# Loading keys and queries in runs of four tokens, and spreading them in SBUF

## The chip, the cores and the metric

The kernel runs on one core of one Trainium2 chip. The metric is device time in microseconds (us) of one execution; a run's time is a little longer than the span of its profile, which goes from the first to the last instruction.

## The reference

An attention with a sliding window and ALiBi biases is followed by a feed-forward block with a squared ReLU. The inputs are float32: q, k, v of shape (8, 8, 576, 64), `w_in` of (512, 2048) and `w_out` of (2048, 512).

```python
scores = scale * np.matmul(q, k.transpose(0, 1, 3, 2))        # scale = 1/8
rel = pos[:, None] - pos[None, :]
bias = slopes[:, None, None] * (-np.abs(rel))[None, :, :]     # slopes = 2 ** -(h + 1)
scores = np.where((rel >= 0) & (rel < 128), scores + bias[None], -1e9)
attn = softmax(scores)
x = (attn @ v).transpose(0, 2, 1, 3).reshape(4608, 512)
out = np.maximum(x @ w_in, 0.0) ** 2 @ w_out
```

## The kernel before

**Tiling.** Each batch's 576 tokens are cut into four blocks of 128 tokens and one of 64, so there are 40 blocks (`seq`). Blocks 0 to 7 are the first blocks of the eight batches; they look at no earlier keys. The output of attention is kept transposed in one tile, `xT`, 512 channels (4 x 128 partitions) by 4608 tokens, in bf16. The feed-forward part works on nine groups of 512 tokens. For group 0, `unit` multiplies one block of 128 tokens by two or four 128-wide pieces of `w_in` at a time (L806, tile `h`); groups 1 and 2 take 256 tokens at a time; later groups take all 512 (`fc_step`, L823). ScalarE applies ReLU (L770, `rt`), VectorE squares (L779, `g`), and `o_piece` (L850, `o`) multiplies by `w_out`.

**A block of attention.** Its keys and queries are loaded into a tile `kq` (128 tokens by 2 x 512, bf16), and its values into `vf` or `vt` (L461). Blocks below N_PE are transposed by TensorE into PSUM (L513, `tp`) and copied to `kqf` by VectorE or ScalarE (the helper `copy`, L304 or L306); the others are transposed by a DMA that SP issues (L499, `kqT`). Scores are L633 for blocks 0 to 3, where biases come first by a matmul (L624), and L572 for the others; ScalarE takes the exponential (L641, L596, tile `P`); L676 multiplies by the values (`pv`), VectorE divides (L693, L702, tile `x`). Blocks below N_XP go into `xT` by a TensorE transpose (L722, `xp`) and a copy, the rest by a DMA transpose on SP (L709).

**Loads.** POOL's DMAs cast float32 to bf16 on the way. Keys and queries of blocks 1 to 39 are loaded token by token and head by head (L456): 64 elements, 256 B of float32, in one run, 1024 runs for 128 tokens. Block 0 goes another way (N_HW = 1): SP and ACT load float32 into a tile `stage` in runs of four tokens of one head (1 KB), and VectorE casts and reorders them into `kq` (`cast_kq`). In that layout a partition holds four consecutive tokens `i` of the two heads `r` of a pair; the transposes' results are then put back into the order of tokens by the copy from PSUM:

```python
src = st.tile[:, 0:512].rearrange("p (i g c) -> p c g i", i=4, c=C)[:, c0:c1]
o = o.rearrange("p c (g i) -> p c g i", i=4)
```

The weights come in five pieces of `w_in` (2, 2, 4, 4 and 4 of 128 columns; i0 to i4 in the list FIRST, L401) and four of `w_out` (o0 to o3, L404). FIRST gives the order in which POOL issues these and the blocks' loads: `k3` is keys and queries of block 3, `v3` its values.

**Order.** Every piece of work is a task with the engines that can do it, a key and the ring buffers it takes. `Plan.order` runs through a cost model of durations and latencies and fixes on which engine, and in which order, each task is emitted; on the chip each engine works through its list in that order and waits by semaphores. ADJ adds offsets to the keys of single tasks, LEAD says how far ahead of need attention blocks are due, SLACK adds reserves to DMA landings, NEAR lets a task with a smaller key pass one that is ready earlier. Where TensorE is expected to wait early on, `fill` puts in matmuls on a tile of zeros (L285), and N_WARM more stand at the start (L483).

Of the kernel before, what the change touches and what calls it, by code (L numbers as in the profile page):

```python
# [13 lines left out]

FIRST = ["k0", "k1", "i0", "v0", "v1", "k2", "v2", "k3", "v3", "i1", "o0", "i2", "i3", "i4", "o1", "o2", "o3", "k4", "k5", "v4", "k6", "k7", "v5", "v6", "v7"]
DIAG = [[0], [1], [2], [3], [4, 5], [6, 7]]
N_HW = 1
N_PE = 8  # L20
N_XP = 8
N_CUT = 0
N_PVH = 2
N_WARM = 8
HALVED = [(7, 1), (7, 2), (7, 3)]
N_EV = 4
SLACK = {"kq": 0.0, "kqT": 4500.0, "v": 2000.0, "x": 2500.0}
FILL = 0.7
LEAD = 1200
IOTA = 3  # L30
TP, XP = "h", "h"

# [5 lines left out]
DUE = {m: 200.0 * m - 1e5 for m in range(40)}  # L38

ADJ = {  # L40
    "b3": 8899994.7, "e13.1": 299208.63, "e14.1": 388.4, "e6.3": -698571.67, "e8.1": 100925.31, "ev1.0.0": 399002.11,
    "ev2.1.2": -197151.21, "fc3.10": -299530.23, "fc3.11": 199489.0, "fc3.13": -99828.3, "fc3.3": -201022.2,
    "fc3.4": -99975.3, "fc3.5": -98590.21, "o0.2.3": -299655.64, "o1.0.1": 99368.6, "o1.0.3": -394556.77,
    "o1.3.0": 199256.6, "o1.3.1": -9000017.0, "o1.3.2": -197810.54, "o1.3.3": 401.7, "o2.0.0": 99409.71,
    "o2.1.0": -790.13, "o2.1.2": -198747.1, "o2.2.2": 603810.31, "o2.2.3": 101596.66, "o2.3.0": -393446.03,
    "o2.3.2": 297555.78, "o3.0.0": 80, "pv20.0": 599.54, "r11.1": -954.05, "r12.0": -864.77, "relufc3.1": -398899.93,
    "reluu0.0.0": -301007.9, "reluu0.0.1": -99855.3, "reluu0.2.0": -197840.0, "reluu2.0.7": 496046.89,
    "s12": -100922.05, "s13": 40, "s17": 1287.08, "s4": -778.4, "s6": -98770.15, "s8": 5078.93,
    "squ0.0.1": -600103.44, "squ0.2.0": -100094.3, "squ1.1.6": -8498736.06, "tp4.0": -2659.55, "u0.0.1": 400493.27,
    "u0.0.2": 200, "u0.0.3": 198055.18, "u1.0.1": -398247.52, "u1.0.4": -955.31, "u1.1.0": -198342.1,  # L50
    "u1.1.2": -296084.77, "u1.1.4": -200120.3, "u1.1.6": -199431.2, "u1.1.7": -8597648.05, "u2.0.0": 393881.15,
    "u2.1.1": -98247.04, "xp7.0": 99135.7,
}


# [23 lines left out]
class Plan:  # L79
# [6 lines left out]
    LAND = {"POOL": 2400.0, "SP": 2200.0, "ACTQ": 900.0}  # L86
    TO_SP = 600.0
    LANES = 8
    NEAR = {"PE": 25, "ACT": 250, "DVE": 0}
    FILL_UNTIL = 30000.0  # L90

    def __init__(self, bufs):
# [114 lines left out]
def kernel(  # L207
# [53 lines left out]
    def ring(name, n, shape, dt=BF16):  # L261
        return [const.tile(shape, dt, name=f"{name}_{i}") for i in range(n)]
# [4 lines left out]
             "kqT": ring("kqT", size["kqT"], [128, 2 * C, 128]), "kqT0": ring("kqf", B, [128, 2 * C, 128])}  # L267
    Pt = ring("P", size["P"], [128, H, 2, 128])
    xt = ring("x", size["x"], [128, d_model])
    stages = ring("stage", min(2, N_HW), [128, 2 * d_model], FP32)  # L270

    psum_bufs = {"h": 2, "o": 2, "a": 4}
    plan = Plan({**psum_bufs, "rec": 4, "rt": 3, "g": 2, "osb": 3, "v0": B, "kqT0": B, "stage": 2, **size})

    def bank(slot, name):
        slot.tile = psum.tile([128, 512], FP32, tag=slot.tag, bufs=psum_bufs[slot.tag], name=name)
# [13 lines left out]
    def act(n):  # L290
        return n * 0.832 + 51.0
# [117 lines left out]
        else:  # L409
            t_wout[n] = t  # L410

    s_kq, s_v, t_kq, t_v = {}, {}, {}, {}

    def source(t, m, split=False):
        b, kb = seq[m]
# [5 lines left out]
    def load_block(m, key, v_key=None):  # L421
        kb = seq[m][1]
        n = blk[kb]
        ns = 870.0 * n / 128
        split = m < N_HW
        s_kq[m], s_v[m] = Slot("kq"), Slot("v" if kb else "v0")

        def view(t, i):
            o = t[0:n, i * d_model:(i + 1) * d_model]
            return o.rearrange("s (r e) -> s r e", r=2) if split else o.rearrange("s (h d) -> s h d", h=H)  # L430

        if split:
            s_st = Slot("stage")
            t_l = []
            for i, src in enumerate((k, q)):
                for r, (eng, e) in enumerate((("SP", nc.sync), ("SP", nc.sync) if m else ("ACTQ", nc.scalar))):
                    def fetch(i=i, src=src, r=r, e=e):
                        e.dma_start(view(stages[s_st.idx], i)[:, r], source(src, m, split)[:, :, r])
                    t_l.append(plan.add({eng: 740.0}, key + 0.1 * i, fetch, [], [] if t_l else [s_st], dma=330.0,
                                        lat=(1100.0 if m else 1500.0) + 600.0 * (r if m else i * (1 - r)),  # L440
                                        name=f"l{'kq'[i]}{m}.{r}", after=t_l[0] if t_l else None))

            def cast_kq(i):
                w = slice(i * d_model, (i + 1) * d_model)
                copy((c_k, c_q)[i],
                     kq[s_kq[m].idx][:, w].rearrange("s (i r d) -> s r i d", i=4, d=D),
                     stages[s_st.idx][:, w].rearrange("s (r i d) -> s r i d", r=2, d=D))
            engs = {"DVE": 350.0, "ACT": 480.0} if m else {"DVE": 350.0}
            c_q = None
            c_k = plan.add(engs, key, lambda: cast_kq(0), t_l[0:2], [s_kq[m]], name=f"ck{m}")  # L450
            c_q = plan.add(engs, key, lambda: cast_kq(1), t_l[2:4] + [c_k], [], [s_st], name=f"cq{m}")
            t_kq[m] = [c_k, c_q]
        else:
            def fetch_kq():
                for i, src in enumerate((k, q)):
                    nc.gpsimd.dma_start(view(kq[s_kq[m].idx], i), source(src, m, split))  # L456
            t_kq[m] = [plan.add({"POOL": 1780.0}, key, fetch_kq, [], [s_kq[m]], dma=2 * ns,
                                name=f"lkq{m}", count=2, slack=SLACK["kq"] if m >= N_PE else 0.0)]

        def fetch_v():  # L460
            nc.gpsimd.dma_start(tile_of(s_v[m])[0:n, :, 0:D], source(v, m))  # L461
        l_v = plan.add({"POOL": 890.0}, key + 0.2 if v_key is None else v_key, fetch_v, t_zero if kb == HALF else [], [s_v[m]],
                       dma=ns, name=f"lv{m}", after=t_kq[m][-1] if m >= B else None,
                       slack=SLACK["v"] if m >= B else 0.0)
        t_v[m] = [l_v] + ([t_one["v0", m]] if m < B else [t_one["v", i] for i in range(size["v"])])
# [26 lines left out]
    def transpose_kq(m, due):  # L492
        n = blk[seq[m][1]]
        kb = seq[m][1]
        sT = s_kqT[m] = Slot("kqT" if kb else "kqT0")
        split = m < N_HW
        if m >= N_PE:
            def flip():
                nc.sync.dma_start_transpose(out=tile_of(sT)[:, :, 0:n], in_=kq[s_kq[m].idx][0:n, :])  # L499
            t_f = plan.add({"SP": 1500.0}, due - 60, flip, t_kq[m] + (t_zero if kb == HALF else []), [sT],  # L500
                           [s_kq[m]], dma=1700.0 * n / 128, name=f"kqT{m}", slack=SLACK["kqT"])
            t_kqT[m] = [t_f]
            return
        t_tp, evs = [None, None], [[], []]
        for i in range(2):
            st = Slot(TP if m else "o")

            def tp(i=i, st=st):
                fill(t_tp[i], bank_of(st, "tp"))
                st.tile = st.tile.bitcast(BF16)  # L510
                src = kq[s_kq[m].idx][:, i * d_model:(i + 1) * d_model]
                for j in range(C):
                    nc.tensor.transpose(st.tile[:, j * 128:(j + 1) * 128],  # L513
                                        src[:, j * 128:(j + 1) * 128], ident)
            t_tp[i] = plan.add({"PE": 4 * mm(128)}, due - 60 + i, tp,
                               [t_ident, t_tp[0] if i else last["tp"], t_kq[m][min(i, len(t_kq[m]) - 1)]],
                               [st] if i else [st, sT], [s_kq[m]] if i else [], name=f"tp{m}.{i}")

            pieces = [(0, C // 2), (C // 2, C)] if m < N_EV else [(0, C)]
            for c0, c1 in pieces:  # L520
                def evac(i=i, st=st, c0=c0, c1=c1, e=len(evs[i])):
                    o = tile_of(sT)[:, i * C + c0:i * C + c1, 0:n]
                    if split:
                        src = st.tile[:, 0:512].rearrange("p (i g c) -> p c g i", i=4, c=C)[:, c0:c1]
                        o = o.rearrange("p c (g i) -> p c g i", i=4)
                    else:
                        src = st.tile[:, 0:512].rearrange("p (c s) -> p c s", c=C)[:, c0:c1, 0:n]
                    copy(evs[i][e], o, src)
                w = (c1 - c0) * n
                evs[i].append(plan.add({"ACT": act(w), "DVE": dve_p(w, 1 if split else 2)}, due - 58, evac,  # L530
                                       [t_tp[i]], [], [st], name=f"ev{m}.{i}.{c0}"))
        last["tp"] = t_tp[1]
        t_kqT[m] = evs[0] + evs[1]
# [384 lines left out]
```

The softmax here doesn't subtract the row's maximum and nothing guards it: scores larger than these inputs give would overflow.

## Time and profile before

| | us |
|---|---|
| four runs, median (lowest to highest) | 313.83 (313.48 to 315.04) |
| the profiled execution | 314.52 |
| its span | 312.7 |
| TensorE busy | 307.0 |
| VectorE, ScalarE, GpSimd busy | 165.8, 169.4, 106.2 |

In the views below, PE is TensorE, PEld its weight loads, DVE VectorE, ACT ScalarE, POOL GpSimd and SP SyncE. A table by windows has for each stretch its length, then the busy time of PE, PEld, DVE, ACT and POOL with the number of instructions in brackets, the granted clock of TensorE, the mean occupancy of the DMA engines (over 1 where packets overlap) and GB/s. A chain of waits has start, length and what ran. A DMA line has the issuing queue, the number of issues, the KB that one writes and the median us from issue to landing; the KB are those of bf16, so that a load reads twice as many.

### The profile page before, as it was taken

Reading aid. Unit: us, or ns where it says so; the run is one execution under the profiler, and the core shown is the slowest. Engines: PE = TensorE matmul, PEld = TensorE weight load, DVE = VectorE, ACT = ScalarE, POOL = GpSimd, SP = SyncE. Lnnn points to the kernel's source line nnn. Section 1 sums busy time; section 2 is a strip of 40 time slices with the busy share of each in tenths; the row PEclk is TensorE's granted clock in tenths of the full one; section 3 lists DMA queues with packets and bytes.
Section 4 is the critical chain, followed back from the end, with each engine's and each line's share of the span. In section 5 each row is a group of like instructions: output and inputs, shape, how many; then the busy total and the mean of one; then the engine's idle time right before and its main releaser. Section 6 shows DMA issues by size and latency. Waiting matters only on the chain.

```text
span 312.7 us, 7098 instructions
## 1 busy us (share of the span) xinstructions
PE 307.0 (98%) x2792; PEld 175.0 (56%) x2792; DVE 165.8 (53%) x496; ACT 169.4 (54%) x324; POOL 106.2 (34%) x132
## 2 busy tenths in 40 slices
PE   8999999999999999999999999999999999999996
PEld 4579757686686844555455554555444444444443
DVE  5664357367667546878677665878222222222211
ACT  2686445486685545864597756665443443434400
POOL 8933596364660943703737364000000000000000
PEclk9999999999999999999999999999999999999999
DMA  9999999999999999998999999941110100011122
GB/s 129 162 205 206 174 194 171 155 141 165 172 188 163 143 173 198 148 125 175 140 179 157 170 163 175 193 78 52 52 34 38 63 36 34 36 36 34 34 85 84
DMA packets 166290, 39.54 MB, mean 126 GB/s; under 512 B 156400, under 2 KB 161776, under 8 KB 166256
## 3 DMA queue, kind: packets, MB, share of 16 engines
q0 software_dynamic: 115184, 18.10, 86.0%
q1 hardware_dynamic: 50640, 20.65, 37.4%
q8 instruction: 22, 0.36, 0.5%
q10 hardware_dynamic: 432, 0.33, 0.4%
q14 instruction: 12, 0.10, 0.1%
HBM read 36.70 MB, written 9.44 MB: 148 GB/s over the span
## 4 chain that ended last, share of the span: by engine, by line
PE 90%; DMA 4%; POOL 4%; issue 0%; ACT 0%; POOLq 0%
PE o L850 40%; PE h L823 27%; PE h L806 12%; PE pv L676 6%; PE s L572 5%; DMA w_in_sb<-in_moe_w_in_dram 4%; POOL kq L456 2%; POOL vf L461 1%; POOL w_in_sb L401 1%; PE tp L513 1%; PE xp L722 0%; POOL w_out_sb L404 0%; POOL dist L320 0%; ACT osb L306 0%; POOLq L320 0%
## 5 line engine op out<-in xcount | busy, mean ns | idle before, releaser
L850 PE MATMUL o<-w_out_sb,g 128*128 128x512 bf16 (+2 forms) x592 | 141.8, 374 | 0.1
L770 ACT ACTIVATE rt<-h 128x512 bf16<-128x512 f32 (+1 forms) x145 | 86.1, 601 | 89.3 <-PE h L823 69.9
L779 DVE TENSOR_TENSOR g<-rt 128x512 bf16<-128x512 bf16 (+1 forms) x145 | 60.4, 419 | 95.8 <-ACT rt L770 95.3
L823 PE MATMUL h<-xT,w_in_sb 128*128 128x512 bf16 x384 | 96.8, 380 | 0.4 <-DMA xT<-x 0.4
L850 PEld LDWEIGHTS <-g 128*128 128x128 bf16 x592 | 54.2, 98 | 57.1 <-issue 0.2
L596 ACT ACTIVATE P<-s 128x512 bf16<-128x512 f32 x120 | 62.2, 607 | 12.9 <-PE s L572 12.8
L823 PEld LDWEIGHTS <-w_in_sb 128*128 128x128 bf16 x384 | 35.4, 98 | 40.4 <-DMA xT<-x 0.5
L456 POOL DMA_DIRECT2D kq<-in_k_dram x39 | 33.6, 861 | 41.5 <-DMA kqT<-kq 31.9
L806 PE MATMUL h<-xT,w_in_sb 128*128 128x128 bf16 (+1 forms) x512 | 46.2, 246 | 0.1
L604 DVE TENSOR_TENSOR P<-P,masks 128x512 bf16<-128x512 bf16 x96 | 38.6, 419 | 11.6 <-ACT P L596 9.1
L806 PEld LDWEIGHTS <-w_in_sb 128*128 128x128 bf16 x512 | 39.0, 98 | 5.5 <-DMA w_in_sb<-in_moe_w_in_dram 0.3
L461 POOL DMA_DIRECT2D vt<-in_v_dram x32 | 27.3, 853 | 32.8 <-PE pv L676 31.7
L456 POOL DMA_DIRECT2D kq<-in_q_dram x39 | 33.6, 860 | 9.1 <-DMA w_out_sb<-in_moe_w_out_dram 3.7
L702 DVE TENSOR_TENSOR x<-pv,rec 128x256 bf16<-128x256 f32 (+1 forms) x80 | 32.1, 418 | 0.8
L676 PEld LDWEIGHTS <-P 128*128 128x128 bf16 (+1 forms) x576 | 24.2, 101 | 11.3 <-DVE g L779 1.3
L676 PE MATMUL pv<-vt,P 128*128 128x65 bf16 (+1 forms) x448 | 22.8, 194 | 0.0
L304 DVE COPY osb<-o 128x512 f32<-128x512 f32 (+1 forms) x19 | 13.0, 685 | 17.2 <-PE o L850 12.0
L306 ACT ACTIVATE osb<-o 128x512 f32<-128x512 f32 (+1 forms) x18 | 10.4, 579 | 21.5 <-PE o L850 21.5
L572 PEld LDWEIGHTS <-kqT 64*128 64x128 bf16 x448 | 12.4, 94 | 7.6 <-issue 7.2
L693 DVE RECIPROCAL rec<-pv 128x4 f32<-128x4 f32 (+1 forms) x80 | 12.4, 172 | 6.2 <-PE pv L676 5.4
L572 PE MATMUL s<-kqT 64*128 64x128 bf16 (+1 forms) x256 | 15.6, 210 | 0.0
L572 PE MATMUL s<-kqT,kqT 64*128 64x128 bf16 (+1 forms) x192 | 11.4, 210 | 0.0
(46 smaller groups left out, 104.7 us busy)
## 6 DMA issues: line engine op xcount, KB each, us to landing
out_dram<-osb SPq DMA_DIRECT2D x28, 256.0 KB, 5.4
kq<-in_k_dram POOLq DMA_DIRECT2D x31, 128.0 KB, 7.0
kq<-in_q_dram POOLq DMA_DIRECT2D x31, 128.0 KB, 7.5
vt<-in_v_dram POOLq DMA_DIRECT2D x24, 128.0 KB, 7.6
w_out_sb<-in_moe_w_out_dram POOLq DMA_DIRECT2D x4, 512.0 KB, 17.3
out_dram<-osb SPq DMA_DIRECT2D x14, 128.0 KB, 2.3
w_in_sb<-in_moe_w_in_dram POOLq DMA_DIRECT2D x3, 512.0 KB, 13.4
vf<-in_v_dram POOLq DMA_DIRECT2D x8, 128.0 KB, 7.0
```

The costliest lines, as they stand in the source:

```text
L456: nc.gpsimd.dma_start(view(kq[s_kq[m].idx], i), source(src, m, split))
L461: nc.gpsimd.dma_start(tile_of(s_v[m])[0:n, :, 0:D], source(v, m))
L572: nc.tensor.matmul(sS[2 * g2 + r].tile[:, jj * 256 + c0:jj * 256 + c0 + w], tile_of(s_kqT[mk])[rows, c, :], tile_of(s_kqT[mq])[rows, C + c ...
L596: nc.scalar.activation(flat(Pt[sP.idx]), sS[i].tile.rearrange("p (j t) -> p j t", j=2)[:, :, lo:hi], AF.Exp, bias=0.0, scale=scale)
L604: nc.vector.tensor_tensor(flat(Pt[sP.idx]), flat(Pt[sP.idx]), flat(masks), op=ALU.mult)
L676: nc.tensor.matmul(sv.tile[0:n, hi * (D + 1):(hi + 1) * (D + 1)], prob, tile_of(s_v[mk])[:, h, 0:D + 1], start=mk == parts[0][1], stop=mk ...
L702: nc.vector.tensor_tensor(o, heads(sv)[0:n, :, 0:D], sr.tile[0:n, :].unsqueeze(2).to_broadcast([n, 4, D]), op=ALU.mult)
L770: nc.scalar.activation(srt.tile[:, 0:n], slot.tile[:, 0:n], AF.Relu, bias=0.0, scale=1.0)
L779: nc.vector.tensor_tensor(o, i, i, op=ALU.mult)
L806: nc.tensor.matmul(slot.tile[:, f * w:(f + 1) * w], w_in_sb[:, cc, fc * 128:(fc + 1) * 128], xT[:, cc, lo:lo + w], start=cc == 0, stop=cc ...
L823: nc.tensor.matmul(slot.tile, w_in_sb[:, cc, fc * 128:(fc + 1) * 128], xT[:, cc, g * 512:(g + 1) * 512], start=cc == 0, stop=cc == C - 1)
L850: nc.tensor.matmul(slot.tile[:, 0:hi - lo], gt[:, fc, t * 128:(t + 1) * 128], w_out_sb[:, fc, lo:hi], start=fc == 0, stop=fc == FCB - 1)
```

## The change

Keys and queries of blocks 1 to 7 (N_ROW = 8) are loaded by POOL in runs of four tokens of one head, 1 KB of float32 each, 256 runs for a block's keys and 256 for its queries. They land as bf16 in columns of `xT` from 1536 on, which attention writes later (`rows_of`), and VectorE or ScalarE copies them to `kq` in two spreads of 128x512 (`spread`). Block 0's `stage` is also laid into `xT`. The copies from PSUM of blocks 1 to 5 now put tokens back in order, as block 0's do. N_PE goes from 8 to 6, so that blocks 6 and 7 are transposed by DMA. That transpose keeps the order by groups of four tokens and head pairs, and nothing behind it puts the tokens of blocks 6 and 7 back: the scores of these two blocks are taken between tokens and heads in another order, with the same shapes and instructions. The order of the first loads, SLACK, LEAD, NEAR, ADJ and two counts (N_EV, how many early blocks have their copies from PSUM halved; N_PVH, how many blocks keep `pv` in the `h` banks) are also different.

```diff
-FIRST = ["k0", "k1", "i0", "v0", "v1", "k2", "v2", "k3", "v3", "i1", "o0", "i2", "i3", "i4", "o1", "o2", "o3", "k4", "k5", "v4", "k6", "k7", "v5", "v6", "v7"]
+FIRST = ["k0", "v0", "k1", "k2", "i0", "i1", "v1", "v2", "k3", "i2", "i3", "v3", "o0", "o1", "i4", "o2", "k4", "o3", "k5", "k6", "v4", "k7", "v5", "v6", "v7"]
-N_PE = 8
+N_PE = 6
+N_ROW = 8
-N_PVH = 2
+N_PVH = 1
-N_EV = 4
-SLACK = {"kq": 0.0, "kqT": 4500.0, "v": 2000.0, "x": 2500.0}
+N_EV = 3
+SLACK = {"kq": 0.0, "kqT": 4000.0, "v": 1000.0, "x": 3000.0}
-LEAD = 1200
+LEAD = 480
 ADJ = {
...
-    NEAR = {"PE": 25, "ACT": 250, "DVE": 0}
+    NEAR = {"PE": 0, "ACT": 60, "DVE": 25}
...
-    stages = ring("stage", min(2, N_HW), [128, 2 * d_model], FP32)
+    def stage():
+        return xT[:, 0, NT - 4 * d_model:].bitcast(FP32)
+
+    def rows_of(m, i):
+        c, z = (m % 3 + 1, m // 3) if m < 6 else (0, 2)
+        end = NT - (2 * z + 1 - i) * d_model
+        return xT[:, c, end - d_model:end]
...
-        split = m < N_HW
+        split = m < N_ROW
...
+        elif split:
+            def fetch_rows():
+                for i, src in enumerate((k, q)):
+                    nc.gpsimd.dma_start(rows_of(m - 1, i).rearrange("s (r e) -> s r e", r=2), source(src, m, split))
+            t_l = plan.add({"POOL": 1560.0}, key, fetch_rows, [], [s_kq[m]], dma=1320.0, name=f"lkq{m}", count=2)
+
+            def spread(i):
+                copy(t_kq[m][i],
+                     kq[s_kq[m].idx][:, i * d_model:(i + 1) * d_model].rearrange("s (i r d) -> s r i d", i=4, d=D),
+                     rows_of(m - 1, i).rearrange("s (r i d) -> s r i d", r=2, d=D))
+            t_kq[m] = []
+            for i in range(2):
+                t_kq[m].append(plan.add({"DVE": dve(512, 2), "ACT": act(512)}, key, lambda i=i: spread(i),
+                                        [t_l] + t_kq[m][:1], name=f"c{'kq'[i]}{m}"))
...
-        split = m < N_HW
+        split = m < N_ROW
         if m >= N_PE:
             def flip():
                 nc.sync.dma_start_transpose(out=tile_of(sT)[:, :, 0:n], in_=kq[s_kq[m].idx][0:n, :])
```

## The prediction

> **What bounds the kernel now.** I read the page first: who is busy, and when.
>
> ```profile
> PE 307.0 (98%) x2792; PEld 175.0 (56%) x2792; DVE 165.8 (53%) x496; ACT 169.4 (54%) x324; POOL 106.2 (34%) x132
> ...
> PE   8999999999999999999999999999999999999996
> ```
>
> TensorE is the bound from end to end, at a clock of 1.0 throughout, so time can only come from work that TensorE no longer does or from time that it spends idle or on filler at the start. The table by windows says where that is, first for all of TensorE, then for the filler of L285 alone:
>
> ```profile
> 10.00:14.00 4.00, 3.46 (x50) 2.43 (x49) 3.14 (x11) 1.72 (x4) 4.00 (x7) 1.00 2.43 154
> 14.00:18.00 4.00, 3.66 (x52) 2.49 (x51) 2.30 (x9) 3.78 (x12) 2.78 (x4) 1.00 1.58 195
> 18.00:22.70 4.70, 4.60 (x64) 3.53 (x62) 3.58 (x20) 3.96 (x15) 1.93 (x3) 1.00 1.24 206
> ...
> 100.00:295.00 195.00, 194.61 (x1586) 98.86 (x1586) 102.14 (x297) 107.50 (x196) 48.21 (x59) 1.00 1.00 108
> ...
> 10.00:14.00 4.00, 1.23 (x13) 0.76 (x13) 1.00 2.43 154
> ```
>
> Behind 100 us only 0.4 us is idle, ahead of the tail. Early "busy" flatters, since the modelled ends overlap, so I count work instead: instructions times the step of a dense run, from the chain that ended last:
>
> ```profile
> 26.56 6.43 PE h L806 x112
> 32.99 0.86 PE o L850 x4
> ...
> 38.23 0.45 PE tp L513 x8
> ...
> 42.58 0.55 PE s L572 x16
> ...
> 46.84 0.37 PE pv L676 x12
> ```
>
> That is 57 ns for an `h` of 128 columns, 216 for a 512-wide `o` or bias, 56 for a transpose, 34 for a score, 31 for a `pv`. By the timeline of TensorE, these were issued before 12.36 us: 16 transposes of keys and queries (0.90), 6 biases (1.30), 16 scores (0.55), 16 pv (0.50), 4 transposes of x (0.22), in all 3.5 us; 8.9 us were lost. From 12.36 to 22.70, where the first long run of `h` begins: 16 tp (0.90), 2 biases (0.43), 16 s (0.55), 16 pv (0.50), 12 xp (0.67), 48 h (2.75), 8 o (1.72), in all 7.5 of 10.3 us; 2.8 us were lost. From 22.70 TensorE runs dense.
>
> What it waits for there is data. The chain is POOL issuing loads without a gap from 1.34, and then a load:
>
> ```profile
> 13.11 13.40 DMA w_in_sb<-in_moe_w_in_dram
> 26.52 0.04 issue
> 26.56 6.43 PE h L806 x112
> ```
>
> **The change, part by part.** *Size of the row loads.* The DMA views of short windows give single landings:
>
> ```profile
> w_in_sb<-in_moe_w_in_dram POOLq DMA_DIRECT2D x1, 256.0 KB, 5.8
> ...
> kq<-in_q_dram POOLq DMA_DIRECT2D x1, 128.0 KB, 5.1
> ...
> w_in_sb<-in_moe_w_in_dram POOLq DMA_DIRECT2D x1, 256.0 KB, 7.3
> vf<-in_v_dram POOLq DMA_DIRECT2D x1, 128.0 KB, 7.1
> ```
>
> With issue starts of 3.23, 2.36, 10.91 and 10.04, the two small w_in pieces land 1.52 and 1.07 us after the load ahead of them. They are written in the runs of 512 B that the new loads would have, and carry twice the data: 0.54 to 0.76 us for a key or query load. Today's land 0.83 to 0.84 apart. POOL's issue is 0.77 for such a w_in piece against 0.87 to 0.95 for a kq load, so issue alone would hold loads to 0.77. I take 0.76: 0.08 us for each of six early loads, 0.5 us in all; the other end is 0.3 each, 1.8 us. The Trainium skill (DMA: Bandwidth & Descriptors, section "Why small descriptors are slow") charges a fixed few cycles for each descriptor; my estimate from its formula is 0.66 us for a load, which would double the 0.5.
>
> *Order of the loads.* This is worth more. With 6.68 us for the first landing (as now), 0.76 for a row load, 0.87 for a v, 1.3 for a small w_in (between 1.07 and 1.52) and 2.55 for a large weight piece (w_in 2 lands at 23.26, 2.55 behind w_out 0), the new list lands: v0 6.7, k1 and q1 8.2, k2 and q2 9.7, i0 11.0, i1 12.3 (now 18.2), v1 13.2 (now 10.8), v2 14.1 (13.3), q3 15.6 (15.0), i2 18.2 (23.3), i3 20.7 (26.5), v3 21.6 (17.1), o0 24.1 (20.7). Block 0 is no earlier: its x waits for q0, which comes by SP and ACT as now, so the 8.9 us stay. From 12.4 TensorE has 16 h for block 0 in place of 8, and at 13.2 + 2.6 = 15.8 block 1's x (from vf's landing at 10.77 to the end of x's copy at 13.9 it is 3.1 now, partly waiting for engines). Between 12.4 and 15.8 the work is 16 h, 4 tp, 8 s, 2 biases, 16 pv: 2.4 of 3.4 us. From 15.8 to 18.2 there are 32 h, 8 xp, 8 tp, 8 s and 2 biases: 3.4 us for 2.4. With i2 at 18.2 it stays dense: 48 h (2.7 us) carry it past i3 at 20.7, and 48 more to 24.6, past o0. So 1.0 us is lost by this count; I take 1.4, because engines will not be free at each moment. Gain 2.8 - 1.4 = 1.4 us; ends 0 and 2.8. What is late next is block 3's x (v3 at 21.6 plus 3), covered by the 96 h of i2 and i3, and behind 24.1 by w_out 0's parts.
>
> *N_PE 8 to 6.* Blocks 6 and 7 lose 16 transposes on TensorE: 16 x 56 ns = 0.9 us, and every one lies in dense time. In their place SP issues two DMA transposes, landing 6.8 us later in the median, 10.5 at worst before 70 us. With q7 landing near 41 they are there by 52; from scores to x takes 5.6 us now (49.1 to 54.7), so 58, and u1.1 needs them near 62 (64.5 now). Cost nothing; without that cover of 4 us, what is missing. On SP the stores of the first group queue behind them: three osb buffers hold that.
>
> *Spreads.* 14 copies of 128x512 bf16, SBUF to SBUF. Nearest rows: 602 ns for VectorE's cast of the same layout from f32, 597 for ScalarE's copy, 417 for VectorE's bf16 copy from PSUM, 272 for a memset with no input. I take 0.42: 2.5 us for the six early ones, ends 1.6 and 3.6. The evictions of blocks 1 to 3 also scatter: 425 ns on VectorE, as block 0's do, for 280 to 290 now; at most 12 x 0.14 = 1.7. Between 5 and 20 us VectorE idles 5.7 us and ScalarE 5.7 (busy 9.3 of 15 each), so I cost both at nothing on the path: k2 and q2 come 2.7 us earlier. Without that cover it is the slower rival below.
>
> *Spreads against POOL.* Beside VectorE's cast (6.28 to 6.89) POOL's issue took 0.93, its neighbours 0.92 to 0.96, a quiet one 0.87: so 0.06 us lost each, 0.4 for six, under the rounding of my loss. The Trainium skill (SBUF — State Buffer, section "Who interferes with whom") speaks against this change: a VectorE copy in a two-port mode shuts GpSimd out for its whole length. By that rule six spreads could hold up issues by 2.5 us and take the early gain.
>
> *LEAD, SLACK, NEAR, ADJ, N_EV, N_PVH.* They only reorder. They can win at most the 0.4 us of idle time; the longest late TensorE wait is 0.4 us (for x by DMA transpose), and four like it would cost 1.6. Taken as 0.
>
> Sum: 1.4 + 0.9 = 2.3 us. The profiled execution took 314.52 us for a span of 312.7, and 313.83 is the median; its span would become 310.4, the median 313.83 - 2.3 = **311.5**.
>
> **The rivals.** *B, the order gives nothing back:* v1 comes 2.4 us later, so block 1 is late and i1 has only block 0 to feed. For it: block 0 and 1 alone fill 12 to 16 us. Then only the transposes count: 313.83 - 0.9 = 312.9 (312.3 to 314.2).
>
> *C, slower: VectorE and ScalarE become the bound from 8 to 20 us.* ScalarE is already busy 3.78 of 4 us from 14 to 18. Spreads and scattered evictions (2.5 + 1.7 = 4.2 us) land in the chain of each block. Shared by both engines and all on the path they cost 2.1 us, in one queue 4.2; with no early gain and less the 0.9 this is 1.2 to 3.3 us, 315.0 to 317.1, middle 316.1. It decides once block 2's x copy, which starts at 18.22 now, starts after 20.
>
> *D, the run is not merged:* packets stay as small as now, rows land 0.83 apart, and only order and transposes count: 0.5 less, 312.0.
>
> **How the numbers follow.** My forecast 0.62 (its own range 309.6 to 312.3), B 0.19, C 0.15, D 0.04. A measurement can tell about 0.5%, 1.6 us, from no change: faster is below 312.3, slower above 315.4. The forecast and half of D are faster, 0.64; B and the rest of D and a little of C within, 0.22; most of C slower, 0.14. For 8 in 10 the range runs from 309.4 (2.8 + 0.9, and the idle 0.4 with rounding) to 315.4, where C's lower part is in.
>
> **What would show it.** Right: the first long run of h starts near 18 us in place of 22.70, filler behind 12 us is nearly gone, L513 has 48 transposes in place of 64, kq loads land below 0.8 us apart, TensorE is still at 1.00 with under 1 us of idle time after 30 us. Wrong: x copies of blocks 1 and 2 behind 16 and 18 us, POOL's issues over 1.1 us beside spreads, or new TensorE waits for kqT or x by DMA after 50 us.

## The result, and the profile after

The kernel after takes 315.10 us in the median of 38 runs (313.48 to 319.10), the kernel before 313.42 in 57 (312.94 to 315.75). The ratio, in which strongly disturbed runs are left out, is 1.0045, with an interval of 1.0033 to 1.0058: slower by 0.45%, a small change, but one that its interval sets apart from none. The forecast was 311.5.

The profiled execution took 314.79 us for a span of 312.56. Its page, the lines of busy time and of TensorE in 40 slices:

```profile
PE 305.4 (98%) x2754; PEld 173.4 (55%) x2754; DVE 171.7 (55%) x502; ACT 170.2 (54%) x326; POOL 103.9 (33%) x132
...
PE   8799999999999999999999999999999999999995
```

TensorE has 38 instructions fewer (16 transposes and 22 fillers), and its first slices are not fuller than before. The same stretches as before, by windows (columns: length, then the busy time of PE, PEld, DVE, ACT and POOL with counts, PEclk, DMA share, GB/s):

```profile
4.58:10.00 5.42, 4.42 (x41) 3.20 (x40) 2.70 (x14) 1.91 (x5) 5.42 (x8) 1.00 1.52 186
10.00:14.00 4.00, 3.36 (x48) 2.56 (x48) 2.63 (x8) 2.92 (x7) 3.75 (x5) 1.00 1.85 177
14.00:18.00 4.00, 3.36 (x52) 2.19 (x50) 3.30 (x13) 3.94 (x14) 2.18 (x4) 1.00 1.25 206
18.00:22.70 4.70, 4.65 (x81) 4.16 (x79) 2.14 (x15) 4.35 (x16) 2.14 (x3) 1.00 1.46 198
```

The DMAs move more (206 for 195 GB/s from 14 to 18 us), but TensorE is busy for less. ScalarE has 3.94 of 4 us from 14 to 18.

**The data did come earlier.** The early row loads land 0.67 to 0.73 us apart (forecast 0.76, before 0.83). The second small piece of `w_in`, i1, lands at 12.16 us (forecast 12.3, before 18.21), i2 at 18.44 (18.2; 23.26), i3 at 20.60 (20.7; 26.52). All of this part of the forecast held.

**TensorE did not gain by it.** By 30 us both profiled executions have begun the same work: 174 `h`, 8 `o`, 32 transposes of keys and queries, 16 of x, 8 biases, 32 scores and 32 `pv`. The rows of `h` up to 30 us, before and after (count, then busy us, mean ns, idle us before):

```profile
L806 PE MATMUL h<-xT,w_in_sb 128*128 128x128 bf16 x174 | 10.5, 219 | 0.1
```

```profile
L830 PE MATMUL h<-xT,w_in_sb 128*128 128x128 bf16 x174 | 11.1, 219 | 0.2
```

Counted as in the prediction (instructions times the step of a dense run), TensorE has then lost 11.8 us in both: in the kernel after 0.4 more between 5 and 10 us, 0.6 less between 10 and 15, and 0.4 more between 15 and 20. Up to 30 us no load is on the chain that ended last. Pieces of it (start, length, what ran):

```profile
9.22 0.24 PE tp L537 x4
9.46 0.02 issue
9.48 0.44 DVE kqf L314
9.92 0.02 issue
9.94 0.39 ACT kqf L316
10.33 0.04 issue
10.37 0.29 PE pv L700 x4
```

Block 1's first transposes, then the two halves of their copy one behind the other, then the second `pv` of block 0: TensorE stands 0.73 us for ScalarE's half. The transposes take a bank of `h`, which has two, and with N_PVH = 1 block 0's `pv` takes the next from there; a bank comes free when its last half is copied.

**Balance of the two profiled executions.** TensorE ends at 309.38 in place of 309.83: 0.9 us of transposes less, 0.45 more lost in small pieces from 30 to 240 us. From the last matmul to the end of the span it is 3.18 us, before 2.83; outside the span 2.23, before 1.86. So -0.45 + 0.35 + 0.37 = 0.27, and 314.79 - 314.52 is 0.27. The medians lie further apart (1.7 us) because the runs of the kernel after spread more: a quarter lie below 314.08 and a quarter above 316.04 (before 313.22 and 313.91). Before's profiled execution was one of its long ones. Of the 38 runs 26 have a mean granted clock above 0.998, and their median is 314.3 us; the other 12 have 316.9. So about half of the 1.7 us is there at full clock too: 0.9, of which 0.35 is the tail and 0.4 the time outside the span.

### The profile page after: what moved, and what is told of

It is laid out like the page before. It is cut to its first block, busy times and chain, and to the rows that moved or that the text cites. A ratio compares the mean times of both kernels' runs of the same rounds, so it can differ in the third digit from the quotient of the medians.

```text
span 312.6 us, 7033 instructions
## 1 busy us (share of the span) xinstructions
PE 305.4 (98%) x2754; PEld 173.4 (55%) x2754; DVE 171.7 (55%) x502; ACT 170.2 (54%) x326; POOL 103.9 (33%) x132
## 4 chain that ended last, share of the span: by engine, by line
PE 93%; DMA 3%; ACT 2%; DVE 1%; issue 0%
PE o L874 38%; PE h L847 27%; PE h L830 14%; PE pv L700 6%; PE s L596 5%; DMA xT<-x 3%; PE wm L507 1%; ACT kqf L316 1%; DVE kqf L314 1%; PE tp L537 1%; PE xp L746 0%; PE s L648 0%; PE tp L295 0%; ACT P L665 0%; PE s L657 0%; ACT masks L354 0%
## 5 line engine op out<-in xcount | busy, mean ns | idle before, releaser
L628 DVE TENSOR_TENSOR P<-P,masks 128x512 bf16<-128x512 bf16 x96 | 40.0, 421 | 15.4 <-ACT P L620 11.6
L480 POOL DMA_DIRECT2D kq<-in_k_dram x32 | 26.9, 840 | 54.2 <-DMA kqT<-kq 44.5
L700 PEld LDWEIGHTS <-P 128*128 128x128 bf16 (+1 forms) x576 | 23.2, 100 | 11.0 <-ACT P L665 1.0
L480 POOL DMA_DIRECT2D kq<-in_q_dram x32 | 27.2, 849 | 0.9 <-DMA vt<-in_v_dram 0.8
L700 PE MATMUL pv<-vt,P 128*128 128x65 bf16 (+1 forms) x448 | 21.5, 194 | 0.0
L314 DVE COPY osb<-o 128x512 f32<-128x512 f32 (+1 forms) x18 | 12.3, 683 | 13.4 <-PE o L874 9.8
L596 PEld LDWEIGHTS <-kqT 64*128 64x128 bf16 x448 | 12.4, 94 | 7.8 <-issue 7.4
L717 DVE RECIPROCAL rec<-pv 128x4 f32<-128x4 f32 (+1 forms) x80 | 12.4, 172 | 6.6 <-PE pv L700 5.7
```

The costliest lines, as they stand in the source:

```text
L596: nc.tensor.matmul(sS[2 * g2 + r].tile[:, jj * 256 + c0:jj * 256 + c0 + w], tile_of(s_kqT[mk])[rows, c, :], tile_of(s_kqT[mq])[rows, C + c ...
L628: nc.vector.tensor_tensor(flat(Pt[sP.idx]), flat(Pt[sP.idx]), flat(masks), op=ALU.mult)
L700: nc.tensor.matmul(sv.tile[0:n, hi * (D + 1):(hi + 1) * (D + 1)], prob, tile_of(s_v[mk])[:, h, 0:D + 1], start=mk == parts[0][1], stop=mk ...
```

## The experiments

The theory after the result (*S*): the early gain was spent on the way to TensorE, in spreads and scattered copies. Rivals: the order of the loads, the DMA transposes of blocks 6 and 7, and the later order of tasks.

**With a new plan.** In the first four kernels the planner makes a new order for each setting.

*Rows and spreads, but the lists and knobs of before:*

```diff
-FIRST = ["k0", "v0", "k1", "k2", ...
+FIRST = ["k0", "k1", "i0", "v0", ...
-N_PE = 6
+N_PE = 8
...
```

(and so N_PVH, N_EV, SLACK, LEAD, NEAR and ADJ)

> The changed kernel's row loads and spreads, with every list and knob of the kernel before (FIRST, N_PE = 8, N_PVH, N_EV, SLACK, LEAD, NEAR, ADJ). Before is 313.4 us, after 315.1. Theory S (spreads and scattered copies from PSUM lengthen each early block's chain, so that TensorE loses what the earlier data gave): 314 to 315.5, with block 1's first transpose of keys over 1 us later than the 7.6 us of before. Theory O (the new order and knobs cost the time, the rows themselves help): 312.5 to 313.4. Theory C (in some runs TensorE's clock is halved for a window, for want of filler): runs with a mean clock below 1.000 appear only where filler is much less than the 40 instructions of before.

320.46 us, ratio 1.022 (1.0204 to 1.0235). A wait of 1.2 us for x by DMA transpose opens; it ends at 89.6 us.

*After with tokens in place of rows:*

```diff
-N_ROW = 8
+N_ROW = 1
```

> The changed kernel with N_ROW = 1: token by token loads as before, no spreads, and transposes of blocks 6 and 7 by DMA in the order of tokens; all other lists and knobs as after. Theory S: at or below before, 312.3 to 313.4, since the new order keeps its 1.4 us and N_PE = 6 its 0.9. Theory O: as after, 314.5 to 315.5. Theory C: follows the number of filler matmuls, not the loads.

324.61 us, 1.0359 (1.0342 to 1.0376).

*After with eight blocks transposed by TensorE:*

```diff
-N_PE = 6
+N_PE = 8
```

> The changed kernel with N_PE = 8, so that TensorE transposes blocks 6 and 7 and their tokens stand in order. By my price for 16 transposes in dense time it is 0.9 us slower than after (316.0). If instead the DMA transposes cost more than they save, it is 315.1 or less.

323.02 us, 1.0304 (1.0288 to 1.032). Up to 30 us its TensorE loses what after's does (11.8 us). Behind that, as in the token kernel, waits open from 83 to 85 us on, the longest for x (2.0 us, up to 90.1, here), and the clock is halved (from 89.0 to 95.8 us here). For the token kernel, first the longest wait of TensorE (us in total, times, longest), then its windows, the clock third from the end:

```profile
PE h L830 <- DMA xT<-x: 3.4, 1, 3.4
```

```profile
84.00:88.00 4.00, 2.64 (x43) 1.64 (x41) 3.26 (x10) 3.34 (x7) 2.84 (x4) 1.00 3.32 111
88.00:99.00 11.00, 7.23 (x61) 4.81 (x62) 4.53 (x13) 4.39 (x8) 3.31 (x4) 0.53 1.71 174
```

*The kernel just above without spreads* (`t_kq[m] = [t_l]`): the transposes read the rows where they landed, 64 columns for each head:

```diff
+                    if N_HW <= m < N_ROW:
+                        for r in range(2):
+                            at_c = r * 256 + j * D
+                            nc.tensor.transpose(st.tile[r * D:(r + 1) * D, j * 128:(j + 1) * 128],
+                                                rows_of(m - 1, i)[:, at_c:at_c + D], ident)
```

> As e3, but without the 14 spreads: each 128x128 transpose of blocks 1 to 7 becomes two of 64 columns that read the landed rows in place, 112 in place of 56. Theory S: below e3 by 1 us or more, less 0 to 1.6 us for the added transposes (28 to 56 ns each), so 314 to 315.5, with block 1's first transpose at most 0.7 us behind the landing of its keys. Theory O: no better than e3, 316 or above.

318.01 us, 1.0154 (1.0128 to 1.018). A pair of 64-column transposes takes the 56 ns of one of 128, but what follows a group of them starts later. The group and the next instruction, in this kernel and in the kernel after:

```profile
16.47 0.41 PE L533 MATMUL tp<-ident,xT 128*64 128x128 bf16 x8
16.82 0.30 PE L699 MATMUL pv<-vf,P 128*128 128x65 bf16 x4
```

```profile
16.44 0.39 PE L537 MATMUL tp<-ident,kq 128*128 128x128 bf16 x4
16.67 0.59 PE L648 MATMUL s<-slopes,ident 128*128 128x512 bf16 x2
```

That is 0.35 us for 0.23, some 0.12 us for each group, which the expectation of a later kernel without spreads takes for nothing. What follows from the four: ADJ and the lists fit one plan only; another plan costs 4.6 to 11 us against the kernel before, over half of it lost between 80 and 100 us (2.9 to 9.9 us by the count above, where before loses 0.1). They say little of rows and spreads, so the next kernels hold the order of every task and change only what a task issues.

**With the order held.** *After's order, token loads, no spreads, plain copies:*

```diff
-                    nc.gpsimd.dma_start(rows_of(m - 1, i)..., source(src, m, split))
+                    nc.gpsimd.dma_start(kq[s_kq[m].idx][:, i * d_model:(i + 1) * d_model]..., source(src, m))
             def spread(i):
-                copy(...)
+                pass
```

> After's order of every instruction on every engine kept as it is; only what is emitted differs: keys and queries of blocks 1 to 7 come token by token into kq, no spreads, copies from PSUM dense (so blocks 6 and 7 keep the order of tokens). e1 to e3 let the planner order anew and lost 5 to 11 us, most of it near 85 to 95 us, so order has to be held. Theory S (spreads and scattered copies eat what the earlier data gives): 314.0 to 315.1, the start of h for 8 to 10 us of feed-forward work within 0.5 us of after's 18.8 to 19.1. Theory R (row loads are needed for this order): that start moves past 20 us and the time to 316 or more.

316.97 us, 1.0115 (1.0088 to 1.0141), some 1.9 us above the kernel after. But the early part is not where they go. `w_in` lands later (i2 at 19.16 for 18.44, i3 at 21.66 for 20.60), and TensorE stands 0.4 us for i2 and 0.5 us for v3; the plain copies (0.36 us, below) and a start 0.14 us earlier offset part of this. In sum it is not behind. The same run of `h` starts, here and in the kernel after (counts up to 30 us):

```profile
27.44 2.73 PE L829 MATMUL h<-xT,w_in_sb 128*128 128x128 bf16 x46
```

```profile
27.48 2.73 PE L830 MATMUL h<-xT,w_in_sb 128*128 128x128 bf16 x46
```

So up to there the rows with all that goes with them gain nothing over tokens, and Theory R's late start does not come. Behind it this profile has one long wait of TensorE, up to 86.8 us; why it is there is not shown:

```profile
PE h L829 <- DMA xT<-x: 2.3, 1, 2.3
```

*After's order, no spreads for blocks 1 to 5*, 64-column transposes as above:

```diff
             def spread(i):
+                if m < N_PE:
+                    return
```

> After's order kept; the ten spreads of blocks 1 to 5 are left out, and TensorE transposes the landed rows in pieces of 64 columns (28 ns each in e4, so no dearer). Blocks 6 and 7 as in after. Theory S: 0.5 to 1.5 us below after, 313.6 to 314.6, and the time outside the span, 2.2 us in the three kernels with spreads and 1.8 in the three without, falls back to 1.8. If spreads lie beside other work: 315.1 as after.

315.20 us, 1.0058 (1.0034 to 1.0081): not faster. TensorE's waits (engine, tile and line; us in total, times, longest) are those of the kernel after (0.7, 0.5 and 0.5):

```profile
PE pv L708 <- ACT kqf L316: 0.7, 1, 0.7
PE s L665 <- DVE kqf L314: 0.5, 1, 0.5
PE pv L708 <- ACT P L673: 0.5, 1, 0.5
```

Its shortest run is longer than after's (314.91 for 313.48), about by what its ten groups of 64-column transposes add (1.2 us at 0.12 each). So leaving the spreads out leaves TensorE's waits as they are: they are not on after's path, and that part of *S* falls.

*Before's order with rows, and VectorE spreads just ahead of the transposes;* the copies from PSUM of blocks 1 to 7 scatter, here and in the next kernel:

```diff
+                    if m < N_ROW:
+                        nc.gpsimd.dma_start(rows_of(m - 1, i)..., source(src, m, True))
...
+                if N_HW <= m < N_ROW:
+                    nc.vector.tensor_copy(kq[s_kq[m].idx]..., rows_of(m - 1, i)...)
```

> Before's order kept; keys and queries of blocks 1 to 7 come in runs into xT, VectorE spreads each just ahead of its transposes, copies from PSUM scatter. Theory S: 0.5 to 2 us slower than before, 313.9 to 315.4. Theory O (only the new order costs): at or below before, 312.6 to 313.4, by 0.5 us of earlier landings.

318.41 us, 1.0145 (1.0121 to 1.017).

*Before's order with rows, no spreads:* the first of these two edits, scattered copies, and 64-column transposes as above.

> As f3 without spreads, transposes by 64 columns from the landed rows. Theory S: faster than f3 by 0.5 to 1.5 us and than before by 0 to 0.7 us, 312.7 to 313.4; only the scattered copies are left as a cost. Theory O: as f3.

314.88 us, 1.0038 (1.0025 to 1.005). In before's order the spreads stand in the way and cost at least 3.5 us (the difference of the two). Without them the rows bring `w_in` 1.6 to 2.0 us earlier (i1 at 16.42 for 18.21, i3 at 24.72 for 26.52), and the kernel is still slower than before. Of that, some 1.0 us is the price of its eight groups of 64-column transposes, and its scattered copies cost something too, so the time alone does not tell what the rows are worth. The start of the first long run of `h` does: 22.86 us, where the two profiles of the kernel before have 22.70 and 22.27. Four of the eight groups stand ahead of it (0.5 us); even without them earlier `w_in` would bring it no gain that is clear of this spread. Block 0's queries by SP land at 6.54 here, 6.18 before.

*Before's order, blocks 6 and 7 by DMA transpose in place of TensorE's:*

```diff
             def tp(i=i, st=st):
+                if m in (6, 7):
+                    if i:
+                        nc.sync.dma_start_transpose(out=tile_of(sT)[:, :, 0:n], in_=kq[s_kq[m].idx][0:n, :])
+                    return
```

> Before's order kept, token loads; only blocks 6 and 7 are transposed by DMA where their TensorE transposes and copies stood (two DMAs more on SP). By my price 0.9 us of TensorE time go, less 0.35 us at the end, where two DMAs more turn the order in which SP waits for its last DMAs (after's profile has 3.18 us from the last matmul to the end of the span, before's 2.83): 312.9. If the transposes by DMA come too late for their place in the order: 314 or more, with TensorE waiting for kqf by DMA near 45 to 52 us.

321.75 us, 1.0257 (1.0229 to 1.0285).

```profile
PE s L578 <- DMA kqf<-kq: 5.6, 2, 3.1
```

Two waits, from 48.3 and 51.7 us on, and half clock from 50.7 to 57.5. At the place that the transposes had on TensorE, the DMA's are too late; after's own order issues them early enough and shows no such wait.

**How far executions of one kernel differ.** *Before again:*

> The kernel before, unchanged, for another profile: the first one took 314.52 us with a span of 312.7, where most runs of it have spans of 311.4 to 312.0. I expect 311.6, with the end of TensorE's work near 308.8 in place of 309.83. If the other profile is typical after all, 312.7.

313.24 us; TensorE ends at 308.64, 1.2 us earlier than in the first profile.

*After again:*

> The changed kernel, unchanged: more runs with their granted clock, and another profile. Theory C: some of the runs again have a mean clock of 0.994 to 0.995 or 0.988 and are 1 to 3 us longer, the others have spans of 311.3 to 313.3; runs of before stay at 1.000. If it is a matter of the chip alone: all at 1.000 and one span.

315.37 us (313.83 to 319.49), 1.0046 (1.0024 to 1.0069). Its profiled run is its longest. First its waits, then its windows:

```profile
PE h L847 <- DMA xT<-x: 2.7, 1, 2.7
```

```profile
119.00:123.00 4.00, 1.27 (x14) 0.70 (x12) 1.53 (x6) 0.60 (x1) 0.36 (x1) 1.00 1.47 138
123.00:126.50 3.50, 3.50 (x24) 1.46 (x21) 0.43 (x1) 1.22 (x3) 0.00 (x0) 0.51 2.27 123
```

At group 3's first `fc` TensorE waits for x, 0.4 us in the profiles of before and after, and 2.7 here. A window of 3.4 us at half clock follows. The Trainium skill (TensorE: Matmul & The Clock Gate, section "What's actually happening") has the clock drop after an idle window of about 3.4 us, and the window free-running. Here the half clock lasts 3.4 us, but the idle time before it is 2.7 us, shorter than such a window, and idle times of 2.7 and 2.3 us at the same place in two kernels below cost no clock; so the length of an idle time alone does not say here what it costs.

*After with halved stores in groups 4 and 5*, to change the number of DMAs that SP waits for at the end; some of these stores write other rows:

```diff
-HALVED = [(7, 1), (7, 2), (7, 3)]
+HALVED = [(7, 1), (7, 2), (7, 3)] + [(g, t) for g in (4, 5) for t in range(3)]
```

> After, with six stores of groups 4 and 5 cut in halves, so that the number of SP's DMAs is again that of before modulo eight. If the order of SP's last waits costs 0.35 us in after, its median falls by 0.35, to 314.7, and the time from the last matmul to the end of the span falls from 3.18 to 2.83. If not: 315.1 and 3.18.

314.62 us, 1.0046 (1.0019 to 1.0073). The tail is 3.27 us. The edit overshot: SP issues 118 DMAs here, 111 in the kernel after and 109 in the kernel before, and 117 would have given before's remainder by eight. The traces show what the tail is even so. At the end SP waits for eight semaphores in a fixed order, one behind the other, and the last landing of a store comes 1.91 to 1.92 us after the last matmul in all three. In before one of SP's waits ends behind it, in after seven do, here eight, 0.06 us apart, and SP is through at 1.99, 2.35 and 2.43 us. That is the 0.35 us of after's tail, and it comes with the two DMAs more.

**Three more questions.** *Before with 14 more copies on VectorE behind 240 us*, two in each of seven tiles of groups 6 and 7:

```diff
+            for _ in range(2 if g in (6, 7) and len(extra) < 14 else 0):
+                extra.append(g)
+                nc.vector.tensor_copy(kq[0][:, 0:512].rearrange("s (i r d) -> s r i d", i=4, d=D),
+                                      kq[1][:, 0:512].rearrange("s (r i d) -> s r i d", r=2, d=D))
```

> The kernel before with 14 more copies of 128x512 (bf16, SBUF to SBUF, the layout of the spreads) on VectorE behind 240 us, where nothing waits for them; what they write is not read again. It asks what the time outside the span is, 1.78 us in the kernel before and 2.2 in the kernel after. If it goes with the number of such copies: span as before, 311.5 to 312.5, time less span 2.2, ratio 1.0013. If it goes with the loads or the order: time less span 1.78, ratio 1.000.

313.71 us, 1.0011 (0.9991 to 1.0031). Outside the span it is 1.98 us in the median: half of the way from 1.78 to 2.2, so neither theory is right. Its profile shows that the kernel before too can stand at 119 us:

```profile
PE h L824 <- DMA xT<-x: 2.7, 1, 2.7
```

So this wait is no property of the change. The clock stayed at 1.00.

*After without the entry for group 3's first `fc`:*

```diff
-"fc3.0": -17901147.64,
```

> The kernel after without one entry of ADJ, that of the first fc of group 3, so that this matmul keeps its place behind the work that is ready; the order differs only near 119 us. Theory: TensorE stands there for x by a DMA transpose, 0.4 us in a good execution and 2.9 in a bad one, and the bad ones lose another 1.7 us in a window of half clock. Then the wait is gone, the clock is 1.00 in most runs, the median falls by about 0.5 us to 314.6 and the highest run lies below 316. Rival: the late transpose stops TensorE somewhere else as well, and median and spread are those of the kernel after, 315.1 and 313.5 to 319.

315.09 us (313.85 to 317.54), 1.005 (1.0028 to 1.0073). The wait is gone from its profile, but four of twelve runs still have a mean clock of 0.989 or 0.995, and the median is that of the kernel after. The theory falls.

*After with the transposes of blocks 4 and 5 done twice:*

```diff
+                    for _ in range(2 if m in (4, 5) else 1):
-                    nc.tensor.transpose(st.tile[:, j * 128:(j + 1) * 128],
-                                        src[:, j * 128:(j + 1) * 128], ident)
+                        nc.tensor.transpose(st.tile[:, j * 128:(j + 1) * 128],
+                                            src[:, j * 128:(j + 1) * 128], ident)
```

> The kernel after with every transpose of blocks 4 and 5 done twice into the same place: 16 more on TensorE, as many as the change took off it. It prices them. If TensorE is dense there and nothing gives the time back, the span grows by 0.9 us and the median is 316.0. If what TensorE gains is lost to waits behind it (x at 119 us), those waits shorten by as much, and the median is 315.1 to 315.4 with fewer runs above 316.

315.33 us, 1.0065 (1.0042 to 1.0088). A quarter of its runs lie below 315.12, of after's below 314.08, and the spans of its six shortest runs are 312.8 to 313.1, of after's fourteen shortest 311.3 to 312.1. That is about the 0.9 us of the forecast; in the medians the spread blurs it to 0.2. Its profiled run is a long one again, for another reason. First TensorE's waits, then the timeline (start, busy time, what ran, idle time before it), then windows:

```profile
PE tp L538 <- DVE kq L314: 1.9, 1, 1.9
```

```profile
5.55 0.83 PE L295 MATMUL tp<-warm 128*128 128x128 bf16 x12
8.28 0.40 PE L538 MATMUL tp<-ident,kq 128*128 128x128 bf16 x4 [1.90 <-DVE kq L314]
```

```profile
8.00:10.00 2.00, 1.18 (x13) 0.72 (x14) 1.28 (x10) 0.38 (x1) 1.56 (x3) 0.66 1.36 170
10.00:12.00 2.00, 1.62 (x11) 0.96 (x11) 0.56 (x3) 1.19 (x3) 2.00 (x3) 0.50 1.74 181
```

SP's load of block 0's queries landed at 7.71 us, where it took 5.94 in the profile of after. TensorE ran out of filler, and the clock was halved until about 15 us.

*After with plain copies from PSUM in blocks 1 to 5:*

```diff
-                    if split:
+                    if m < N_HW:
                         src = st.tile[:, 0:512].rearrange("p (i g c) -> p c g i", i=4, c=C)[:, c0:c1]
```

> The kernel after with the copies from PSUM of blocks 1 to 5 in the plain layout (0.28 us for a half in place of 0.42), so that the tokens of these blocks stay in groups of four and their scores are taken in another order; all else as it is. Theory: the early bound is the chain of TensorE, VectorE and ScalarE through these copies; four halves lie in the chain of each of blocks 1 and 2, two of them one behind the other, and the loss of TensorE by 30 us falls from 12.2 by 0.3 to 1.0, median 314.1 to 314.8. Rival: the loss is elsewhere (clock, landings, exponentials), and it stays at 12.2 and the median at 315.1.

315.28 us, 1.0058 (1.0032 to 1.0084). In the time nothing is seen. In the trace it is, since after's start is a rigid chain: from the transposes of block 0's queries to the first long run of `h`. Timelines of the kernel after, after again, after without `fc3.0`, and with plain copies:

```profile
7.08 0.39 PE L537 MATMUL tp<-ident,kq 128*128 128x128 bf16 x4
...
19.45 3.11 PE L830 MATMUL h<-xT,w_in_sb 128*128 128x128 bf16 x48
```

```profile
7.85 0.40 PE L537 MATMUL tp<-ident,kq 128*128 128x128 bf16 x4 [0.61 <-DVE kq L314]
...
20.23 3.11 PE L830 MATMUL h<-xT,w_in_sb 128*128 128x128 bf16 x48
```

```profile
6.54 0.40 PE L537 MATMUL tp<-ident,kq 128*128 128x128 bf16 x4 [0.38 <-DVE kq L314]
...
18.92 3.11 PE L830 MATMUL h<-xT,w_in_sb 128*128 128x128 bf16 x48
```

```profile
7.10 0.39 PE L537 MATMUL tp<-ident,kq 128*128 128x128 bf16 x4
...
19.12 3.11 PE L830 MATMUL h<-xT,w_in_sb 128*128 128x128 bf16 x48
```

It takes 12.37, 12.38 and 12.38 us wherever it starts, and 12.02 with the shorter copies. So the stretch goes through the copies from PSUM (0.36 us of it by their layout). What sets its place in time differs. In the second and third TensorE waits for block 0's queries (0.61 and 0.38 us). In the first and last it does not: these queries landed at 5.94 and 6.06 us, but the 12 fillers ahead were issued 107 ns apart, where in the third they were 56 apart, and lasted longer.

*After with 22 fillers ahead of these transposes in place of 12, and before with 12 in place of 22:*

```diff
+        more = 10 if task.name == "tp0.1" else 0
-        for _ in range(int(task.gap * FILL / 56.0) if task.gap > 200.0 else 0):
+        for _ in range(int(task.gap * FILL / 56.0) + more if task.gap > 200.0 else 0):
```

> The kernel after with ten more filler matmuls ahead of the transposes of block 0's queries, 22 as in the kernel before in place of 12; all else as it is. Theory: block 0's last load of queries lands anywhere between 5.9 and 7.7 us; with 12 fillers TensorE runs out of work near 6.4 to 7.2 us, and where the load is late its idle time drops the clock to a half for 3.4 or 6.8 us. Then with 22 at most 1 run in 12 shows a mean clock below 0.998 (12 of 38 in the kernel after), and the median falls from 315.1 to 314.2 to 314.5, while the lowest runs stay at 313.5 to 313.9. Rival: the half clock comes from waits near 119 us; 3 or 4 of 12 still show it, and the median stays at 315.1.

> The kernel before with ten fewer filler matmuls at the same place, 12 in place of 22. Theory: what the kernel after lacks is this bridge, so the kernel before without it gets its spread: 2 to 5 of 12 runs with a mean clock below 0.998 (none of the runs before), median 313.7 to 314.8, highest run above 316. Rival: the kernel before has other work there (transposes of block 1, whose keys come first in its list), and median and spread stay at 313.4 and 313.0 to 315.

After with 22: 314.99 us (314.15 to 316.83), 1.0046 (1.0029 to 1.0063). None of twelve runs has two windows of half clock, but three have one, and its lowest run lies 0.7 us higher, as the fillers hold up the transposes where the load is early. Before with 12: 314.43, 1.0024 (1.0008 to 1.0039), no run below a clock of 0.998. So the bridge is worth 0.24% to the kernel before (0.9 us, of which 0.3 lie outside the span), but in clock it explains little. No kernel here beats the kernel before.

## Why the prediction was wrong

- **What bounds the kernel now: "What it waits for there is data."** This step failed. The chain of before named a `w_in` load ending at 26.52, but a chain goes back from the last wait, and TensorE had stood 0.29 us for that load. Before it, the 2.8 us were lost in many short waits among transposes, copies, exponentials and `x`. In after's order token loads brought `w_in` 0.7 to 1.1 us later, and TensorE was at the same place at 27.4 us; in before's order rows brought it 1.6 to 2.0 us earlier, and the first long run of `h` started no earlier. In its place the runs show the chain through the copies from PSUM: 12.4 us from block 0's queries to that run in after's order, wherever it starts.
- **Order of the loads, a loss of 1.4 in place of 2.8 us.** This term was wrong for the same reason. All landings came as worked out; the loss by 30 us is 11.8 in both. The sum treated each `h` as ready with its `w_in`, and let the engines add 0.4 us to a count of 1.0. That the 8.9 us of block 0 stay was too kind as well: block 1's transposes come 1.3 us later (9.06 for 7.79), in place of work that stood there before; its keys land at 7.04 for 6.68, and VectorE spreads them from 7.94 to 8.64. The sign named for being right, a first long run of `h` near 18 us, nearly came (19.45) and gained nothing, since less other work stood ahead of it. A sign named for being wrong came: the copies of x of blocks 1 and 2 start at 16.37 and 19.77 us, behind 16 and 18. Rival B named this mechanism, v1 late, and is nearest to what happened, though its 312.9 leaves out all that follows.
- **N_PE, 0.9 us.** Held: doing 16 transposes twice brings back about 1.0 us in the lower quarter of runs. It does not show in the median, because other terms take it. One of them belongs to this term, whose DMAs were to cost nothing: the two more on SP lengthen the tail by 0.35 us.
- **Spreads, nothing on the path.** Held in after's order (no gain without them), not in before's, where they cost at least 3.5 us. Sizes: 0.26 to 0.29 us on VectorE, twice 0.48 and once 0.70, and 0.62 on ScalarE; 0.42 was taken.
- **Spreads against POOL.** POOL's row issues take 0.70 to 0.71 us, with and without a spread beside them. The slowest spread ran while POOL issued, but six others beside issues took 0.26 to 0.29. The Trainium skill (SBUF — State Buffer, "Who interferes with whom") has the shared port lock out the other engine; the 0.43 us of that one spread would fit it as a loss of VectorE's, and no run here separates it.
- **Knobs, 0.** Wrong as a rule: a plan is one fit of lists, ADJ and knobs. In the change itself the later order loses 0.45 us; the kernels with mixed knobs were 4.6 to 11 us slower than the kernel before.
- **Rival C** had the right engines, at the wrong place and with the wrong cause: ScalarE is full from 14 to 18 us, but what binds is the chain through copies, and block 2's copy to `xT` starts at 19.77, short of its point of 20. That its range, 315.0 to 317.1, holds the measured 315.10 is luck: it put 2.1 to 4.2 us of spreads and scattered copies on the path, and the runs show nothing for the spreads and 0.36 us for the copies. **Rival D** fell, as rows land 0.67 to 0.73 us apart.
- **Not foreseen.** The tail (+0.35 us), the time outside the span (+0.37), and the spread. 12 of after's 38 runs have a mean clock of 0.988 to 0.995, none of over 90 runs of the kernel before. Two places were seen where it starts, block 0's queries and x at 119 us; taking away the second, or bridging the first, did not end it. Why this order falls into it and before's does not stays open, and so does the time outside the span: more copies raise it by 0.2 us, but before with 12 fillers, without any, has 1.8 to 3.0. The tail is the order of SP's last waits, as above.

## What to carry to other kernels

A load at the end of a chain is not yet the bound: add up how long the engine stood for it, and try the earlier data alone, with the order held, before counting the gain. Where a planner's offsets are fitted to one order, an experiment that replans measures the plan; change what the tasks issue and leave their order. Such an edit can bring a cost of its own, as the 64-column transposes did: look for it in the trace before reading the difference of two times. Compare lower quarters as well as medians when runs spread, and ask what the start hangs on.

## What the runs showed of the hardware

A wait of TensorE can cost twice: behind idle times of 1.9 and 2.7 us the granted clock was 0.5 for 6.8 and 3.4 us, while other waits of 2.3 and 2.7 us at full clock had no such sequel. The same load of 128 KB by SP landed 4.5 to 6.2 us after its issue in executions of one kernel family, and where the fillers ended sooner, the whole start moved with it. A group of 64-column transposes held up the next instruction by some 0.12 us more than one of whole transposes. SP's last waits, behind the last landing, took 0.06 us each, and which of them were left over followed from the number of DMAs that it had issued. The time outside the span differed by up to 1.3 us between runs of one kernel.
